# Plain-fp32 first units, a PE-built bias, a GpSimd causal mask and PE-made weight halves in an attention + maxout kernel

## The chip, the cores and the metric

One core of one Trainium2 chip runs the whole program in one launch. The metric is device microseconds of that core, as the median of several executions. Engines are written as in the profile: PE (TensorE matmul; PEld its weight loads), DVE (VectorE), ACT (ScalarE), POOL (GpSimd), SP (SyncE, which here issues nearly all DMAs).

## What is computed

Causal attention with a forget-gate bias for 8 batches of 8 heads, 576 positions of width 64, followed by a maxout feed-forward over 4608 tokens:

```
cum   = cumsum(max(s, 0))
bias  = min(-(cum[i] - cum[j]), 0)
score = q @ k.T / 8 + bias, and -1e9 where j > i
attn  = softmax(score);  x = attn @ v        # heads side by side: 4608 x 512
h     = max(x @ w1, x @ w2, x @ w3)          # 512 -> 768
out   = h @ w_out                            # 768 -> 512
```

The inputs q, k, v and s arrive as fp32; the weights arrive as float64 and are brought to fp32 words on the chip.

## The kernel before

**Units and steps.** Heads are handled in pairs `g` (four pairs per batch). The query rows of a batch are cut in five blocks `qb` (four of 128 rows and one of 64). A unit is a group of steps: "split" units (batches 0 to 3, two pairs, `qb` 0 and 1), "rest" units (the same batches, one pair, `qb` 2 to 4) and "whole" units (batches 4 to 7, one pair, all five). There are 8, 16 and 16 of them, 160 steps in all. Units 0 and 1 together make the first 256 rows of batch 0, and with them the first input `x` of the feed-forward.

**One step** (`one_step`, L727). PE forms the scores of both heads as three products of rounded parts, `qh·kh + ql·kh + qh·kl` (L752, fp32r), and adds the causal mask with one more matmul per head, `identb` times `tri` (L756). DVE subtracts the bias and takes the row minimum in one instruction (L796); ACT takes the exponential and the row sum (L805); ACT and DVE make the reciprocal (L812, L818). The normalized probabilities are split in two f16 halves, ACT the high one (L841) and DVE the low one (L849). SP transposes them by DMA (L861). After the last step of a phase PE multiplies with the halves of v (L904), and ACT or DVE write the halves of `x` (L930, L932, L937).

**What a unit needs first.** `qk_in` (L640) loads q and k (`qr`), rounds them on ACT (`qh`, L696), subtracts on DVE for the first five units and on POOL later (`ql`, L709), and loads the bias rows (`bias`, L686) spread over all partitions from `cd`, a DRAM copy of the cumulative sums. `cd` is made at the start: load `s` (L303), maximum (L337), scan (L342), centre and scale (L349), write to DRAM (L355). `values_split` (L605) makes the halves of v (ACT L618, DVE L623).

**Weights.** 24 tiles of 128 x 512: 18 for the three up products, 6 for the down product, taken in chunks of three (the last six together). Per tile: one ACT and two DVE instructions that turn the float64 words into fp32 (L423, L427, L431), a share in a Gram product on PE (L446) from which a power of two is derived in a chain of small DVE operations per chunk (L456 to L478), and two f16 halves: the high one by ACT (L514), the low one by DVE (L521).

**Experts** (`experts`, L948). One per batch and phase, 16 in all, each with 18 up groups of 12 matmuls (L981) whose results DVE, ACT and POOL turn into `h` (L992 to L1016), and 4 down groups of 18 (L1037).

**Order.** A planner (`Plan`) holds prices per operation and a key; it simulates the five engines and writes each engine's instruction order from that. Attention steps have the step number as key, weights `PACE[0]*i + PACE[1]`, and the experts a key so large that PE turns to them when no attention work is ready. PSUM holds two score tiles, one `av` tile and three `m` tiles; `p` and `pr` have two buffers each. Every engine runs its list in order; the semaphores follow the true dependences of each instruction. In the planner's own picture every POOL operation, and those of DVE marked as locking, exclude each other.

Of the kernel before, what the change touches and what calls it, by code (L numbers as in the profile page):

```python
# [20 lines left out]
PACE = (1.2, 0.0, 2200.0)  # L21
EARLY = 5
EARLYSET = 0
LOOK = (4.0, 10.0, 3.0, 3.5)
# [28 lines left out]
class Plan:  # L53
# [47 lines left out]
    def run(self):  # L101
# [15 lines left out]
        while left:  # L117
# [9 lines left out]
            for e in engines:  # L127
# [3 lines left out]
                while wait[e]:  # L131
# [4 lines left out]
                    held = pair > now and (e == "POOL" or e == "DVE" and op.lock)  # L136
# [16 lines left out]
                if e == "POOL" or e == "DVE" and op.lock:  # L153
                    pair = op.end
                    heapq.heappush(events, (pair, 1, 0, None))
# [27 lines left out]
def kernel(  # L183
# [8 lines left out]
    nc = tc.nc  # L192
# [26 lines left out]
        sc=6, am=3, vs=5, ws=3, os=4, s=2, av=1, m=3,  # L219
# [72 lines left out]
    ident = inner("ident", 16 * S, 4 * P)  # L292
# [27 lines left out]
    def do(e):  # L320
        nc.gpsimd.memset(tri4(), 0.0)
        for j in range(2):
# [8 lines left out]
        {"DVE": dve(128)},  # L331
        lambda e: nc.vector.tensor_scalar(out=identb(), in0=ident(), scalar1=1.0 / VSC, scalar2=None, op0=ALU.mult),
        -1000.0, [ident], [identb],
    )
    add(
        {"DVE": (451.0, 370.0)},
        lambda e: nc.vector.tensor_scalar(out=rt_()[0:HB], in0=st()[0:HB], scalar1=0.0, scalar2=None, op0=ALU.max),  # L337
        -1000.0, [st], [rt_],
    )
    add(  # L340
        {"DVE": (1350.0, 1270.0)},
        lambda e: nc.vector.tensor_tensor_scan(  # L342
            out=ct()[0:HB], data0=rt_()[0:HB], data1=rt_()[0:HB], initial=0.0, op0=ALU.add, op1=ALU.max
        ),
        -1000.0, [rt_], [ct],
    )
# [40 lines left out]


# [11 lines left out]
    def weights(c):  # L400
# [80 lines left out]
        if c == NFT:  # L481
# [23 lines left out]
            )  # L505
        for i in ids:
# [12 lines left out]

            def lo(e, r=r, w=w, sc=sc):  # L520
# [10 lines left out]
    units = [("split", b, (2 * h, 2 * h + 1), (0, 1)) for b in range(NB) for h in range(NP // 2)]  # L531
    units += [("rest", b, (g,), (2, 3, 4)) for b in range(NB) for g in range(NP)]
    units += [("whole", b, (g,), (0, 1, 2, 3, 4)) for b in range(NB, B) for g in range(NP)]
# [71 lines left out]
    def values_split(u):  # L605
        kind, b, gs, qbs = units[u]
        n = 512 if kind == "split" else 640
        rv, vs = RV.pop(u), VS[b, kind]
# [31 lines left out]
    def qk_in(u):  # L640
# [3 lines left out]
        hi = buf("qh", name=f"qh{u}")  # L644
        lo = buf("ql", name=f"ql{u}")
        bias = buf("bias", name=f"bias{u}")
        QK[u] = dict(lo=lo, hi=hi, bias=bias)
# [33 lines left out]
        def spread(e):  # L681
# [8 lines left out]
        load(  # L690
            spread, k - LOOK[2], 4 * P * nb_ * rows_, [cd], [bias], queue="ACT" if u == 0 else "SP", lat=2500.0,
        )
        for part, c0, c1 in parts:
# [37 lines left out]
    def one_step(u, a, g, qb, t, r, part, pT, tT):  # L731
        kind, b, gs, qbs = units[u]
        hi = lambda: r["hi"]().bitcast(F32R)
        lo = lambda: r["lo"]().bitcast(F32R)
        if kind == "split":
            qo, ko = 512 * a, 512 * a + 256
        else:
            qo, ko = 0, QP
# [4 lines left out]
        def scores(e):  # L743
            ps = sp().rearrange("p (a n) -> p a n", a=2)
            h, l = hi(), lo()
            if qb < 4:
                qs = slice(qo + qb * P, qo + qb * P + P)
                ks = slice(ko, ko + nk)
                for n, (lt, rt) in enumerate(((h[:, qs], h[:, ks]), (l[:, qs], h[:, ks]), (h[:, qs], l[:, ks]))):
                    for j in range(2):  # L750
                        rs = slice(D * j, D * j + D)
                        nc.tensor.matmul(  # L752
                            ps[:, j, :nk], lhsT=lt[rs], rhs=rt[rs], start=(n == 0), stop=False, skip_group_check=True
                        )
                for j in range(2):
# [16 lines left out]
        cost = (606.0, 673.0, 848.0, 1019.0, 938.0)[qb]  # L772
        add(
            {"PE": (cost + 100.0, cost)}, scores, t, [(r["hi"], part), (r["lo"], part), identb, tri, tri4], [sp]
        )
# [14 lines left out]

        for j in range(2):
# [5 lines left out]
                    out=pj(c)[rs], in0=src(c)[rs], in1=bias(j)[rs], scale=-SCALE, scalar=3.0e38, op0=ALU.add,  # L797
# [322 lines left out]
```

## Time and profile before

| | us |
|---|---|
| median of 3 executions (lowest, highest) | 856.57 (855.74, 857.03) |
| the profiled execution: its time | 857.28 |
| its span | 855.5 |
| PE busy | 808.5 (95%) |
| DVE busy | 603.5 (71%) |
| ACT busy | 544.5 (64%) |
| POOL busy | 168.3 (20%) |

The profile was taken in one execution whose time stands 1.8 us above its span. "Busy" is the union of the instructions of an engine; because matmuls are pipelined, a run of them is better read by the distance from one start to the next than by the mean of one.

### The profile page before, as it was taken

The numbers are of one execution on the slowest core, as the hardware profiler recorded it, in microseconds if no ns is written. First come the engines' busy times: TensorE is split into PE (matmuls) and PEld (weight loads), VectorE is DVE, ScalarE is ACT, GpSimd is POOL, SyncE is SP. The second block draws the span as 40 slices with busy tenths as digits, with TensorE's granted clock in tenths as the row PEclk, the third lists the DMA queues.
The fourth block names the chain that finished last, engine by engine and source line by source line (L and its number), as shares of the span: only waits on it lengthen the run. The fifth ranks groups of instructions, "written<-read, shape, count | busy, mean of one in ns | idle before, by whom it ended". The sixth has DMA issues, their size and how long they took to land.

```text
span 855.5 us, 19695 instructions
## 1 busy us (share of the span) xinstructions
PE 808.5 (95%) x7251; PEld 618.2 (72%) x7251; DVE 603.5 (71%) x1757; ACT 544.5 (64%) x1422; POOL 168.3 (20%) x177
## 2 busy tenths in 40 slices
PE   2558999999999999999999999999999999999998
PEld 1336878788887776777776788767877778778875
DVE  4998988777787878867767776687768768652221
ACT  3777877777776776776666766667676766751111
POOL 0000322222231312312222222221211222011110
PEclk9999999999999999999999999999999999999999
DMA  9887965899888888887765767676686655440000
GB/s 336 219 222 185 230 165 133 177 203 176 207 178 200 187 196 193 191 215 167 154 147 141 167 133 147 142 149 150 138 172 148 142 121 107 100 76 32 8 19 32
DMA packets 243216, 132.66 MB, mean 155 GB/s; under 512 B 211248, under 2 KB 225584, under 8 KB 243120
## 3 DMA queue, kind: packets, MB, share of 16 engines
q1 hardware_dynamic: 242432, 130.59, 66.7%
q8 instruction: 57, 0.93, 0.5%
q10 hardware_dynamic: 688, 0.82, 0.3%
q14 instruction: 39, 0.32, 0.2%
HBM read 70.40 MB, written 9.58 MB: 93 GB/s over the span
## 4 chain that ended last, share of the span: by engine, by line
PE 87%; DVE 6%; DMA 3%; issue 2%; ACT 1%; ACTq 0%; DVEq 0%
PE u L981 48%; PE d L1037 15%; PE s L752 9%; PE av L904 8%; PE s L764 3%; PE s L756 3%; DVE pr L849 2%; DMA bias<-cd 1%; DMA pT<-pr 1%; DVE p L796 1%; DMA cd<-early 1%; PE m L446 1%; DMA early<-in_s_dram 1%; DVE m L1004 0%; DVE ql L709 0%
## 5 line engine op out<-in xcount | busy, mean ns | idle before, releaser
L981 PE MATMUL u<-x,w 128*128 128x256 f16 (+1 forms) x3456 | 444.8, 287 | 0.1
L981 PEld LDWEIGHTS <-w 128*128 128x128 f16 x3456 | 333.1, 98 | 81.9 <-issue 0.3
L805 ACT ACTIVATE p<-p,sc 128x384 f32<-128x384 f32 (+4 forms) x288 | 166.1, 578 | 80.0 <-DVE sc L796 78.8
L849 DVE SCALAR_TENSOR_TENSOR pr<-p,sc,pr 128x384 f16<-128x384 f32 (+3 forms) x288 | 166.6, 595 | 31.9 <-ACT pr L841 31.0
L1016 POOL TENSOR_TENSOR h<-m,h 128x256 f16<-128x256 f32 (+1 forms) x96 | 72.9, 760 | 514.4 <-ACT h L1011 514.1
L796 DVE CUSTOM_DVE_ANT_0 p<-s,bias 128x512 f32<-128x512 f32 (+4 forms) x320 | 165.3, 537 | 8.0 <-DMA bias<-cd 3.7
L841 ACT ACTIVATE pr<-p,sc 128x384 f16<-128x384 f32 (+3 forms) x288 | 151.4, 568 | 22.1 <-DMA pT<-pr 16.3
L1004 DVE SCALAR_TENSOR_TENSOR m<-u,m 128x256 f32<-128x256 f32 (+1 forms) x192 | 87.3, 455 | 90.3 <-PE u L981 84.5
L1037 PE MATMUL d<-h,w 128*128 128x256 f16 (+1 forms) x1152 | 148.4, 286 | 0.0
L1037 PEld LDWEIGHTS <-w 128*128 128x128 f16 x1152 | 110.6, 98 | 27.0
L709 POOL TENSOR_TENSOR ql<-qr,qh 128x384 fp32r<-128x384 f32 (+2 forms) x70 | 94.0, 1363 | 160.7 <-issue 100.9
L1011 ACT ACTIVATE h<-m 128x256 f16<-128x256 f32 (+1 forms) x96 | 42.2, 439 | 100.3 <-DVE m L1004 99.5
L904 PE MATMUL av<-pT,vv 128*64 128x320 f16 (+3 forms) x1152 | 77.0, 280 | 2.5 <-DMA pT<-pr 2.5
L904 PEld LDWEIGHTS <-vv 128*64 128x64 f16 x1280 | 63.2, 112 | 22.3 <-issue 12.9
L752 PE MATMUL s<-qh 64*128 64x128 f32 (+3 forms) x256 | 55.4, 428 | 17.8 <-ACT qh L696 9.0
L1048 ACT ACTIVATE o<-d,os 128x256 f32<-128x256 f32 (+1 forms) x64 | 31.6, 494 | 47.2 <-PE d L1037 43.8
L996 DVE TENSOR_SCALAR m<-u 128x256 f32<-128x256 f32 (+1 forms) x58 | 26.4, 455 | 42.9 <-PE u L981 41.1
L752 PEld LDWEIGHTS s<-qh 64*128 64x128 f32 x256 | 25.5, 194 | 41.3 <-issue 21.5
L805 ACT ACTIVATION_READ_ACCUMULATOR p<-p,sc 128x1 f32 x288 | 54.1, 188 | 0.0
L696 ACT ACTIVATE qh<-qr 128x960 fp32r<-128x960 f32 (+3 forms) x41 | 43.8, 1069 | 6.3 <-DMA qr<-in_qkv_dram 2.4
L752 PE MATMUL s<-qh,ql 64*128 64x128 f32 (+3 forms) x256 | 43.5, 335 | 2.4 <-DVE ql L709 2.4
L818 DVE RECIPROCAL sc<-sc 128x2 f32<-128x2 f32 (+1 forms) x160 | 25.1, 158 | 28.7 <-ACT sc L812 27.8
(81 smaller groups left out, 655.5 us busy)
## 6 DMA issues: line engine op xcount, KB each, us to landing
bias<-cd SPq DMA_DIRECT2D x32, 576.0 KB, 4.7
rv<-in_qkv_dram SPq DMA_DIRECT2D x32, 320.0 KB, 3.9
qr<-in_qkv_dram SPq DMA_DIRECT2D x16, 608.0 KB, 4.2
raw<-in_w_dram SPq DMA_DIRECT2D x16, 512.0 KB, 5.6
qr<-in_qkv_dram SPq DMA_DIRECT2D x16, 480.0 KB, 3.8
out_dram<-o SPq DMA_DIRECT2D x32, 160.0 KB, 2.1
early<-in_w_dram SPq DMA_DIRECT2D x8, 512.0 KB, 6.3
out_dram<-o SPq DMA_DIRECT2D x32, 128.0 KB, 2.6
```

The costliest lines, as they stand in the source:

```text
L696: lambda e, c0=c0, c1=c1: nc.scalar.activation(out=hi().bitcast(F32R)[:, c0:c1], in_=raw()[:, c0:c1], func=AF.Copy),
L709: lambda e, d0=d0, d1=d1: E[e].tensor_tensor(out=lo().bitcast(F32R)[:, d0:d1], in0=raw()[:, d0:d1], in1=hi()[:, d0:d1], op=ALU.subtract),
L752: nc.tensor.matmul(ps[:, j, :nk], lhsT=lt[rs], rhs=rt[rs], start=(n == 0), stop=False, skip_group_check=True)
L796: lambda e, j=j, rs=rs, c=c: nc.vector.tensor_tensor_reduce(out=pj(c)[rs], in0=src(c)[rs], in1=bias(j)[rs], scale=-SCALE, scalar=3.0e38, o ...
L805: lambda e, j=j: nc.scalar.activation(out=pj(j), in_=pj(j), func=AF.Exp, scale=-1.0, bias=nm()[:, j:j + 1], accum_out=sm()[:, j:j + 1]),
L841: lambda e, h_=h_, s_=s_, j=j: nc.scalar.activation(out=h_(), in_=s_(), func=AF.Copy, scale=ri()[:, j:j + 1]),
L849: lambda e, h_=h_, l_=l_, s_=s_, j=j: nc.vector.scalar_tensor_tensor(out=l_(), in0=s_(), scalar=ri()[:, j:j + 1], in1=h_(), op0=ALU.mult, ...
L904: nc.tensor.matmul(av()[j * D:(j + 1) * D, c0:nq], lhsT=lt, rhs=rt, start=(n < 2), stop=(n >= len(todo) - 2), skip_group_check=True,)
L981: nc.tensor.matmul(pm()[:, :nq], lhsT=v[:, wt, kt, :], rhs=x(xt, kt), start=(k == 0), stop=(k == 3 * NKT - 1),)
L1004: lambda e, pm=pm, m1=m1: nc.vector.scalar_tensor_tensor(out=m1()[:, :nq], in0=pm()[:, :nq], scalar=HSC, in1=m1()[:, :nq], op0=ALU.mult, o ...
L1016: lambda e, m1=m1, ft=ft: E[e].tensor_tensor(out=h(1, ft), in0=m1()[:, :nq], in1=h(0, ft), op=ALU.subtract),
L1037: nc.tensor.matmul(pm()[:, :nq], lhsT=v[:, wt, dt, :], rhs=h(c, ft), start=(k == 0), stop=(k == 3 * NFT - 1))
```

## The change

- **First three units (`ND = 3`) in plain fp32.** Scores are one fp32 product of the raw q and k; there is no `qh`, `ql` or split v for these units. The probabilities stay unnormalized in fp32. POOL makes a diagonal matrix with the reciprocals (`pr = ident * ri`), and PE multiplies each probability block with it, which transposes and normalizes at once; ACT or DVE copies the result from PSUM (`turned`). The product with v is fp32 as well, and its scale goes into the `x` evictions.
- **Bias of units 0 and 1 (`NPB = 2`) by PE.** The scan is cut at column 256; the first 256 columns, centred, are `near`; PE spreads each row over the partitions with a one-column lhsT of `ident`, and ACT copies it. The other units load from `cd` as before.
- **Causal mask from unit 4 on (`MASKU = 4`, `qb < 4`) by GpSimd.** An `affine_select` on POOL writes the masked bias into the `p` tile; L796 then reads it there; the two mask matmuls of the step go.
- **Low halves of weight tiles 6 to 17 (`LOPE`) by PE.** A diagonal of the negated scale times the raw fp32 words, plus the f16 identity times the high half, in one `m` tile; ACT copies it. The DVE instruction L521 of these tiles goes.
- **Orders.** Weights get later keys; q and k are asked for 10 steps ahead instead of 4; the low part of `h` is made by DVE for the first two experts; the small scaling of the sums (L812) may go to DVE; the down groups of the first two output tiles are cut so that the last sixth of `h` is used in a part of its own; unlocked POOL operations no longer exclude others in the planner's picture. `ident` and the new small tiles live in the second `pT1` buffer.

```diff
-PACE = (1.2, 0.0, 2200.0)
+PACE = (1.6, -2.0, 1500.0)
-EARLYSET = 0
-LOOK = (4.0, 10.0, 3.0, 3.5)
+EARLYSET = 2
+LOOK = (10.0, 10.0, 4.0, 1.5)
+ND = 3
+NPB = 2
+MASKU = 4
+LOPE = (6, 18)
...
-                    held = pair > now and (e == "POOL" or e == "DVE" and op.lock)
+                    held = pair > now and op.lock and e in ("POOL", "DVE")
...
+    spans(0, 2 * P)
     add(
+        {"DVE": dve(256, 150.0, 1.0)},
+        lambda e: nc.vector.tensor_scalar(
+            out=near()[0:HB], in0=ct()[0:HB, 0:2 * P], scalar1=ct()[0:HB, P:P + 1], scalar2=1.0 / SCALE,
+            op0=ALU.subtract, op1=ALU.mult,
+        ),
+        -1000.0, [(ct, 0)], [near],
     )
+    spans(2 * P, S)
...
+            if LOPE[0] <= i < LOPE[1]:
...
+                def less(e, r=r, w=w, dg=dg, m=m):
+                    nc.tensor.matmul(m(), lhsT=dg(), rhs=words(r)[0], start=True, stop=False)
+                    nc.tensor.matmul(m(), lhsT=identh().bitcast(F16), rhs=w()[:, 0], start=False, stop=True)
+
+                add({"PE": (1300.0, 1200.0)}, less, k, [r, dg, identh, (w, 0)], [m])
+                add(
+                    {"ACT": act(N, PSI)},
+                    lambda e, w=w, m=m: nc.scalar.activation(out=w()[:, 1], in_=m(), func=AF.Copy, scale=-1.0),
+                    k - 0.3, [m], [(w, 1)],
+                )
+                continue
...
+        if u < NPB:
+            for i in range(0, nb_, 2):
+                m = buf("m", free=True)
+
+                def ones(e, m=m, i=i):
+                    for j in range(2):
+                        r = r0 + i + j
+                        nc.tensor.matmul(
+                            m()[:, j * rows_:(j + 1) * rows_], lhsT=ident()[0:HB, r:r + 1].to_broadcast([HB, P]),
+                            rhs=near()[0:HB], start=True, stop=True,
+                        )
+
+                add({"PE": (1300.0, 1200.0)}, ones, FIRST, [ident, near], [m])
...
+                if direct:
+                    terms = ((h[:, qs], h[:, ks]),)
+                else:
+                    terms = ((h[:, qs], h[:, ks]), (l[:, qs], h[:, ks]), (h[:, qs], l[:, ks]))
...
-                for j in range(2):
+                for j in range(0 if masked else 2):
                     nc.tensor.matmul(
                         ps[:, j, qb * P:nk], lhsT=identb(), rhs=tri(), start=False, stop=True, skip_group_check=True
                     )
...
-        cost = (606.0, 673.0, 848.0, 1019.0, 938.0)[qb]
+        cost = ((380.0, 460.0, 630.0, 800.0, 938.0) if masked else (606.0, 673.0, 848.0, 1019.0, 938.0))[qb]
+        if direct:
+            cost += 54.0 * (qb + 1)
...
+            def mask(e):
+                nc.gpsimd.affine_select(
+                    out=pt().rearrange("p (j n) -> p j n", j=2)[:, :, 0:nk],
+                    in_=r["bias"]()[:, 2 * a * w:2 * (a + 1) * w].rearrange("p (j n) -> p j n", j=2)[:, :, 0:nk],
+                    pattern=[[0, 2], [-1, nk]], compare_op=ALU.is_ge, fill=NEG, base=qb * P, channel_multiplier=1,
+                )
+
+            add({"POOL": (127.0 + 2.6 * nk, 100.0 + 2.6 * nk)}, mask, t - 0.5, [r["bias"]], [(pt, 0), (pt, 1)])
...
+    def turned(t, qb, pt, pr, sc, ri, pT):
...
+                lambda e, j=j: nc.gpsimd.tensor_scalar(
+                    out=pr()[:, j * P:(j + 1) * P], in0=ident(), scalar1=ri()[:, j:j + 1], scalar2=None, op0=ALU.mult
+                ),
...
+                for kb in range(qb + 1):
+                    nc.tensor.matmul(
+                        m()[:, (2 * kb + j) * P:(2 * kb + j + 1) * P],
+                        lhsT=pt()[:, 512 * j + kb * P:512 * j + (kb + 1) * P], rhs=pr()[:, j * P:(j + 1) * P],
+                        start=True, stop=True,
+                    )
+
+            add({"PE": (400.0 * (qb + 1), 350.0 * (qb + 1))}, turn, t, [(pt, j), (pr, j)], [(m, j)])
...
-        cost = 1654.0 if ph else 618.0
+        cost = 1654.0 if ph else 1700.0 if direct else 618.0
...
+            cut = NFT - 1 if dt < 2 else NFT
+            for f0, f1 in ((0, cut), (cut, NFT)):
+                if f0 < f1:
+                    add(
+                        {"PE": (3 * (f1 - f0) * mm + 100.0, 3 * (f1 - f0) * mm)},
+                        lambda e, down=down, f0=f0, f1=f1: down(e, f0=f0, f1=f1),
+                        base + 50 + dt + (2 if dt > 1 or f0 else 0),
```

More of the change, by code (lines that the diff above doesn't have):

```diff
@@ L152, in run @@
                 free[e] = now + busy
-                if e == "POOL" or e == "DVE" and op.lock:
+                if op.lock and e in ("POOL", "DVE"):
                     pair = op.end
@@ L386, in power @@
         )
+    for n in range(2):
+        seed = Buf(plan, "dg", None, "order")
+        seed.ops.extend(near.ops)
     W = {}
@@ L528 @@
         weights(c)
[L531 to L533 removed]
+    units = []
+    for o in ORDER:
+        b = int(o[1])
+        if o[0] == "s":
+            units += [("split", b, (2 * h, 2 * h + 1), (0, 1)) for h in range(NP // 2)]
+        elif o[0] == "r":
+            units += [("rest", b, (g,), (2, 3, 4)) for g in range(NP)]
+        else:
+            units += [("whole", b, (g,), (0, 1, 2, 3, 4)) for g in range(NP)]
     begin = []
@@ L688, in spread @@
                 )
[L690 to L693, printed above, removed]
+        if u < NPB:
+            for i in range(0, nb_, 2):
+                m = buf("m", free=True)
+                def ones(e, m=m, i=i):
[4 more added lines that the diff above has]
+                            rhs=near()[0:HB], start=True, stop=True,
+                        )
+                add({"PE": (1300.0, 1200.0)}, ones, FIRST, [ident, near], [m])
+                add(
+                    {"ACT": act(2 * rows_, PSI)},
+                    lambda e, m=m, i=i: nc.scalar.activation(
+                        out=bias()[:, i * rows_:(i + 2) * rows_], in_=m()[:, 0:2 * rows_], func=AF.Copy
+                    ),
+                    FIRST, [m], [(bias, i)],
+                )
+        else:
+            load(spread, k - LOOK[2], 4 * P * nb_ * rows_, [cd], [bias], lat=4500.0 if u < 4 else 2500.0)
+        for part, c0, c1 in parts if u >= ND else ():
             add(
@@ L734, in one_step @@
         lo = lambda: r["lo"]().bitcast(F32R)
+        direct, masked = u < ND, u >= MASKU and qb < 4
         if kind == "split":
@@ L770, in scores @@
                 )
-        cost = (606.0, 673.0, 848.0, 1019.0, 938.0)[qb]
-        add(
-            {"PE": (cost + 100.0, cost)}, scores, t, [(r["hi"], part), (r["lo"], part), identb, tri, tri4], [sp]
-        )
+        cost = ((380.0, 460.0, 630.0, 800.0, 938.0) if masked else (606.0, 673.0, 848.0, 1019.0, 938.0))[qb]
+        if direct:
+            cost += 54.0 * (qb + 1)
+        ins = [(r["raw"], part)] if direct else [(r["hi"], part), (r["lo"], part)]
+        add({"PE": (cost + 100.0, cost)}, scores, t, ins + [identb, tri, tri4], [sp])
         pt = buf("p", name=f"p{t}")
@@ L809, in one_step @@
             )
+        psc = 1.0 if direct else 1.0 / PSC
         add(
-            {"ACT": (204.0, 110.0)},
+            {"ACT": (204.0, 110.0), "DVE": (145.0, 65.0)},
             lambda e: nc.scalar.activation(
-                out=se()[:, :nj], in_=sm()[:, :nj], func=AF.Copy, scale=1.0 / PSC, bias=EPS / PSC
+                out=se()[:, :nj], in_=sm()[:, :nj], func=AF.Copy, scale=psc, bias=EPS * psc
+            )
+            if e == "ACT"
+            else nc.vector.tensor_scalar(
+                out=se()[:, :nj], in0=sm()[:, :nj], scalar1=psc, scalar2=EPS * psc, op0=ALU.mult, op1=ALU.add
             ),
```

141 lines of the change are left out of this document (105 added, 36 removed).

## The prediction

> **What bounds the kernel now.** I read the slices of the span first, then windows by stage, then the waits and the timeline of the start.
>
> ```profile
> span 855.5 us, 19695 instructions
> ...
> PE   2558999999999999999999999999999999999998
> ...
> DVE  4998988777787878867767776687768768652221
> ```
>
> Forty slices of 21.4 us, busy share in tenths. PE is full from the fifth slice on, and not in the first four; DVE is full in just those. Windows put numbers to it (columns: stretch, length, then busy us and count of PE, PEld, DVE, ACT, POOL, then clock, DMA share, GB/s).
>
> ```profile
> 0.00:25.00 25.00, 6.04 (x39) 3.92 (x39) 12.14 (x33) 8.02 (x18) 1.71 (x11) 1.00 0.93 326
> 25.00:70.00 45.00, 23.63 (x171) 16.11 (x172) 44.13 (x155) 36.27 (x98) 0.00 (x0) 1.00 0.85 219
> ...
> 140.00:745.00 605.00, 602.26 (x5485) 457.88 (x5482) 454.09 (x1278) 424.27 (x1096) 136.62 (x131) 1.00 0.74 163
> ```
>
> So two stages. Up to 70 us PE is busy 29.7 us of 70, while DVE works 44.13 of the 45 us from 25 on: the start is bound by DVE, and before 25 by something else. From 140 to 745 PE is busy 602.26 of 605: there only removed PE work shortens anything. The timeline of the start names the early bound:
>
> ```profile
> 5.39 0.45 DVE L337 TENSOR_SCALAR early<-early 64x576 f32<-64x576 f32 x1 [3.83 <-DMA early<-in_s_dram]
> ...
> 14.68 0.42 ACTq L686 DMA_DIRECT2D bias<-cd  x1
> ...
> 23.08 0.29 DVE L796 CUSTOM_DVE_ANT_0 p<-s,bias 128x128 f32<-128x128 f32 x1 [3.70 <-DMA bias<-cd]
> ```
>
> The sums go to DRAM and back; the first softmax starts at 23.08. On PE the stage ends here (the same rows serve below):
>
> ```profile
> 69.92 2.77 PE L981 MATMUL u<-x,w 128*128 128x256 f16 x12
> ...
> 80.91 0.69 PE L904 MATMUL av<-pT,vv 128*64 128x256 f16 x12
> 81.53 0.33 PE L752 MATMUL s<-qh 64*128 64x128 f32 x2
> 81.69 0.28 PE L752 MATMUL s<-qh,ql 64*128 64x128 f32 x2
> 81.80 0.27 PE L752 MATMUL s<-ql,qh 64*128 64x128 f32 x2
> 82.01 0.28 PE L756 MATMUL s<-tri,identb 128*128 128x128 bf16 x2
> 82.13 1.47 PE L981 MATMUL u<-x,w 128*128 128x256 f16 x12
> ...
> 84.21 1.11 PE L446 MATMUL m<-raw 128*128 128x128 bf16 x8
> ```
>
> The first expert starts at 69.92, when units 0 and 1 (eight steps) have given the first `x`. From then on PE always has expert work. Hence the account: the time is the moment at which the first expert can start, plus the PE work still to be done then, plus the end.
>
> **The change part by part.** The sum is made against the profiled execution (857.28 us, span 855.5), 0.7 above the median of 856.57.
>
> *A. When the first expert starts.* `s` still lands at 5.39. On 256 columns the maximum, scan and centring should take about 1 us, two fp32 products and one ACT copy per pair of rows 2 to 4 us: first softmax near 9.5 instead of 23.08. What DVE then has to do is read from its groups between 23 and 69.9 us (count, busy us, mean ns):
>
> ```profile
> L849 DVE SCALAR_TENSOR_TENSOR pr<-p,sc,pr 128x128 f16<-128x128 f32 (+1 forms) x20 | 8.0, 411 | 0.1
> L796 DVE CUSTOM_DVE_ANT_0 p<-s,bias 128x128 f32<-128x128 f32 (+1 forms) x22 | 6.9, 347 | 3.7 <-DMA bias<-cd 3.7
> L521 DVE SCALAR_TENSOR_TENSOR w<-raw,sws,w 128x512 f16<-128x512 f32 x8 | 5.9, 742 | 0.0
> L709 DVE TENSOR_TENSOR ql<-qr,qh 128x512 fp32r<-128x512 f32 x8 | 5.3, 684 | 0.2 <-ACT qh L696 0.2
> L427 DVE TENSOR_SCALAR early<-early 128x512 int32<-128x512 int32 x11 | 4.6, 416 | 0.0
> L431 DVE SCALAR_TENSOR_TENSOR raw<-raw,early 128x512 int32<-128x512 int32 x5 | 3.4, 689 | 0.1
> ...
> L576 DVE TENSOR_REDUCE am<-rv 128x1 f32<-128x512 f32 x5 | 3.4, 674 | 0.0
> ```
>
> The old stage is 69.92 - 23.08 = 46.8 us of full DVE. Of it go, for good in these units, the low halves of the probabilities (8.0) and of q and k (5.3). Put off by the later keys until after the first `x`: 7 of 11 weight conversions (7 x (0.416 + 0.689) = 7.7), half of the 12 low weight halves (6 x 0.742 = 4.5), 3 of 11 softmax steps (6 x 0.347 = 2.1), two of five maxima (1.3) and two scale chains, by my estimate 1.5. That is 30.4 us less: 16.4. Added: the copies of the transposed blocks, half of them on ACT; the nearest row is an eviction of 256 columns,
>
> ```profile
> L932 DVE TENSOR_SCALAR x<-av 128x256 f16<-128x256 f32 x14 | 5.9, 418 | 3.2 <-PE av L904 3.0
> ```
>
> so 4 pairs x (0.42 + about 0.7) / 2 = 2.2; and the early work that used to lie in the wait before 23.08: of the 12.14 us before 25, some 7 (three conversions, two maxima, a scale, the second half of the scan). Together 25.6 us, so at the earliest 9.5 + 25.6 = 35; with some 5 us for chains that the two `p` buffers don't cover, I take **40**. Gain 29.9. Bounds: 33, if chains are covered, and 55, if PE limits (first rival). ACT loses more than it gains there (qh, high halves of p and v against the bias and pT copies), and was busy 36.27 of 45: cover. DMA: q and k of unit 1 are asked for earlier in the same queue and land ahead of later weights.
>
> *B. PE work that the old kernel had behind it at 69.92 and the new one will not have at 40.* Scores of five more steps (82.13 - 81.53 = 0.60 each, 3.1 with the wider blocks) and Gram products of about five weights (1.11 / 2 each, 2.5). Cost 5.6.
>
> *C. Low weight halves by PE, 12 tiles, nearly all after 40 us, in the PE-bound stage.* Per tile an fp32 product of 512 columns and an f16 one. No plain-fp32 matmul is in the trace. Nearest are fp32r pairs of 512 columns, and mask positions:
>
> ```profile
> 189.06 0.39 PE L752 MATMUL s<-qh,ql 64*128 64x512 f32 x2
> 189.28 0.40 PE L752 MATMUL s<-ql,qh 64*128 64x512 f32 x2
> ...
> 196.63 0.28 PE L756 MATMUL s<-tri,identb 128*128 128x128 bf16 x2
> 196.76 5.40 PE L981 MATMUL u<-x,w 128*128 128x256 f16 x48
> ```
>
> One pass of 512 columns takes 0.22. Lower bound: fp32 goes like fp32r, 0.44 per tile, 5.3 in all. Upper: an fp32 product is four products of halves (the kernel makes three of them), 4 x 0.22 + 0.22 = 1.1, 13.2 in all. I take the upper end, since the planner prices it at 1.2, and where its prices can be compared they are good: 618 ns for `av` against 81.53 - 80.91 = 0.62, 606 for a step against 0.60. Cost 13.5. DVE loses 12 x 0.742, ACT gains about as much; neither is the bound there. The Trainium skill (FP8 and Floating Point Precision, TensorE Precision Notes) says that true fp32 takes four passes through the array; an estimate from it would be the same 13.2, and no run here shows it yet.
>
> *D. Unit 2, direct, after 40 us* (units 0 and 1 lie in A, where PE idles). Per pair: scores +0.16 by the planner; six 128-column fp32 products for turning, 2.1 by the planner, from six single passes (0.7) to four passes each (2.9); `av` 1.7 against 0.62. Two pairs: cost 6.7, bounds 1 to 9. The diagonal on POOL, idle until 75 us, is free.
>
> *E. The causal mask leaves PE.*
>
> ```profile
> L756 PE MATMUL s<-tri,identb 128*128 128x128 bf16 x256 | 38.0, 233 | 0.0
> ```
>
> The 38.0 busy overstates it; start to start the two matmuls take 0.13 (196.63 to 196.76) or 0.12 (82.01 to 82.13). The longer wait ahead of them (81.80 to 82.01 against 0.11 between pairs) belongs to the change from half to full array height; I expect the next `u` to inherit it. Masked steps: 16 in split units, 32 in rest, 64 in whole = 112; gain 112 x 0.13 = 14.6. If the wait goes too, 0.23 each, 25.8. POOL pays instead:
>
> ```profile
> masks.py:199 POOL TENSOR_SCALAR_AFFINE_SELECT early<-early 128x128 f32<-128x128 f32 x1 | 0.3, 292 | 0.1
> L324 POOL TENSOR_SCALAR_AFFINE_SELECT tri<-tri 64x64 bf16<-64x64 bf16 x2 | 0.5, 234 | 0.1
> ...
> L709 POOL TENSOR_TENSOR ql<-qr,qh 128x576 fp32r<-128x576 f32 x32 | 45.2, 1414 | 0.0
> L709 POOL TENSOR_TENSOR ql<-qr,qh 128x384 fp32r<-128x384 f32 x16 | 16.5, 1030 | 67.7 <-issue 40.4 <-ACT qh L696 27.0 <-POOL h L1016 0.3
> ```
>
> By the first two rows 0.9 ns per element over 0.18, 88 us in all; by the last two 2.0 over 0.26, 181 us. With 168 us of its own POOL stays below half; `ql` and `h` queue behind a mask that waits for its `p` buffer, so `h` may come a step late, hidden while PE has other groups.
>
> *F. Weights behind the first expert.* Its 18 up groups ask for tiles faster than DVE delivers them; the gap is filled by C, D and later units. I put 4 us of new PE idling, bounds 0 to 12. The cut down groups, L812's choice and `EARLYSET` change order, not PE work: at 842 us the last down groups follow the last up groups without a gap already, so 0; without that cover a wait of one `h` chain, about 2 us.
>
> Sum: -29.9 + 5.6 + 13.5 + 6.7 - 14.6 + 4 = -14.7. 857.3 - 14.7 = 842.6, as a median about **842**.
>
> **Rivals.**
>
> 1. *Slower: plain fp32 on a slow array binds the start.* Before 75 us PE runs at half rate although the granted clock reads 1.00:
>
> ```profile
> 70.13 2.56 PE u L981 x12
> ...
> 79.67 1.31 PE u L981 x12
> ```
>
> PE work up to the first `x`, at planner prices: bias 4 x 1.2, scores 5.8, turning 4 x 2.1, `av` 4 x 1.7, Gram 3.5, together 29 us; at 2.56 / 1.31 that is 57, from about 7 us on: first expert at 64, time 842 + 24 = 866. It decides from a first expert at 55 on. Against it: an array that is busy without gaps speeds up within 4 us (the two rows), so this limits itself. The Trainium skill (TensorE: Matmul & The Clock Gate, Part 1) says the same, that a sustained busy window releases the full clock. Chance 0.12.
>
> 2. *Slower: the mask holds attention back.* DVE is seen blocked: L849 takes up to 1617 ns at a median of 608.
>
> ```profile
> L849 DVE SCALAR_TENSOR_TENSOR pr<-p,sc,pr x288: 332/608/1617, 27.0 to 761.2; 128x512 f16<-128x512 f32 x48, 128x128 f16<-128x128 f32 x32, 128x256 f16<-128x256 f32 x32, 128x384 f16<-128x384 f32 x32
> ```
>
> The Trainium skill (SBUF — State Buffer, SBUF: two separate sides) makes this an exclusive lock between GpSimd and a DVE operation with two SBUF inputs; the new planner picture leaves the mask out of it. But attention has slack:
>
> ```profile
> 771.26 1.65 PE av L904 x28
> ...
> 782.63 25.69 PE L981 MATMUL u<-x,w 128*128 128x256 f16 x228
> ```
>
> The last `x` is there at 774; its expert starts after 18 of the 19 groups of the last row, at 807. So 33 us may be lost, 0.3 per masked step. At 0.5 per step: 56 - 33 = 23 us, 865. Chance 0.06.
>
> 3. *Weights late.* The last tile's key goes from 27.6 to 34.8, seven steps later, at the rate of 40 to 70 us about 15 to 20 us; if the down groups wait for it for 10 us more, 852. Chance 0.17.
>
> 4. *Cheaper than priced.* The array-height wait goes with the mask (-11), or fp32 costs near one pass (-14 in C and D), or the first expert starts at 33 (-7): 826 to 831. Chance 0.20.
>
> **How the numbers follow.** Forecast (832 to 851) 0.45. Rivals 1 and 2 beyond the range are 0.18; rival 4 reaches to 825, rival 3 to 856. Range 825 to 857. A measurement here can tell about 0.2% (1.7 us). Faster: forecast 0.45, rival 4 0.20, most of rival 3 0.14, the mild part of 1: 0.03, so 0.82; same 0.05; slower 0.13.
>
> **What would show it.** First softmax at 8 to 11 us; first `u` at 33 to 48; DVE still full, POOL not above 350 us; low-half groups on PE about 1.1 us start to start, or near 0.4 if fp32 is cheap; the position of L756 taken by `u` 0.2 after the last pair (wait inherited) or 0.1 (gone); PE still full from 140 to 745. A first `u` after 55, or a PE hole between 90 and 150 or after 745, makes the prediction wrong.

## The result, and the profile after

| | before | after |
|---|---|---|
| median (lowest, highest; runs) | 856.8 (855.74, 857.34; 4) | 836.32 (835.97, 837.25; 4) |
| profiled execution: span | 855.5 | 834.4 |
| PE busy | 808.5 | 818.3 |
| DVE busy | 603.5 | 622.6 |
| POOL busy | 168.3 | 266.7 |

The changed kernel takes 0.9764 of the time of the one before, 95% interval 0.9747 to 0.9781: 20.5 us less, where 14.7 were forecast. The slices of the span, as they were read before:

```profile
span 834.4 us, 19417 instructions
...
PE   7889999999999999999999999999999999999998
...
DVE  5899989788888878877788876877878775774231
```

Each slice is 20.9 us here. In the kernel before PE began with 2, 5, 5 and 8 tenths, beside DVE's 4, 9, 9 and 8; now PE begins with 7, 8 and 8 and is full from the fourth slice on. DVE is as busy as it was, but PE no longer waits beside it. The windows of the changed kernel, in the columns of the prediction's, say the same, and the last two cut the span at the first expert:

```profile
0.00:25.00 25.00, 19.54 (x85) 13.80 (x85) 14.32 (x54) 11.21 (x31) 6.22 (x19) 1.00 0.81 285
25.00:70.00 45.00, 39.81 (x279) 26.83 (x280) 41.33 (x163) 37.74 (x99) 13.69 (x20) 0.96 0.72 234
...
140.00:745.00 605.00, 603.02 (x5373) 456.65 (x5372) 474.82 (x1320) 400.09 (x972) 214.43 (x225) 1.00 0.73 158
```

```profile
0.00:49.58 49.58, 39.76 (x230) 28.04 (x230) 36.98 (x143) 30.76 (x83) 14.82 (x32) 0.97 0.72 245
49.58:834.00 784.42, 778.56 (x6876) 592.04 (x6874) 585.63 (x1699) 494.60 (x1224) 251.88 (x273) 1.00 0.67 149
```

The kernel before, cut at its own first expert:

```profile
0.00:69.92 69.92, 29.60 (x208) 19.95 (x208) 56.19 (x187) 44.21 (x115) 1.71 (x11) 1.00 0.88 258
69.92:855.00 785.08, 778.90 (x7046) 598.25 (x7044) 547.30 (x1571) 500.33 (x1308) 166.63 (x166) 1.00 0.66 146
```

The stage after the first expert's start is 784.42 us long against 785.08, and PE is busy 778.56 of it against 778.90. So as bookkeeping nearly all of the gain (20.3 of the span's 21.1) is the earlier start, 49.58 instead of 69.92, and what was added to PE behind it cancels what was taken away. What the bookkeeping can't say is what each part is worth; the experiments give another picture of that.

The start on the changed kernel's timelines, of PE first and then of ACT and DVE (start, length, operation, and in brackets the idle time ahead and what ended it):

```profile
7.18 7.19 PE L770 MATMUL m<-early 64*128 64x256 f32 x16
...
17.19 3.35 PE L1020 MATMUL m<-pr,p 128*128 128x128 f32 x12
...
24.14 2.05 PE L1020 MATMUL m<-pr,p 128*128 128x128 f32 x12
...
47.75 1.29 PE L1020 MATMUL m<-pr,p 128*128 128x128 f32 x8 [0.29 <-POOL pr L1010]
...
49.58 1.47 PE L1143 MATMUL u<-x,w 128*128 128x256 f16 x12
50.89 1.06 PE L573 MATMUL m<-early,early 128*128 128x512 f32 x2
51.79 0.38 PE L574 MATMUL m<-w,early 128*128 128x512 f16 x1
52.10 0.87 PE L1063 MATMUL av<-pT,rv 128*64 128x256 f32 x8
```

```profile
11.71 0.66 ACT L459 ACTIVATE early<-raw 128x512 f32<-128x512 f32 x1 [1.83 <-DMA raw<-in_w_dram]
...
12.41 0.43 DVE L463 TENSOR_SCALAR early<-early 128x512 int32<-128x512 int32 x1 [4.00 <-ACT early L459]
13.48 0.29 DVE L909 CUSTOM_DVE_ANT_0 p<-s,bias 128x128 f32<-128x128 f32 x1
```

The bias is on the partitions early (8 fp32 products from 7.18 on, which the profile records as two matmuls each, x16; the first copy by ACT at 9.29), yet the first softmax starts at 13.48. DVE stood 4.00 us at L463, a weight conversion that the planner had put ahead of it in DVE's list; L463 waited for ACT's L459, and that for the first weight tile's DMA. An engine that runs its list in order waits for the first item of it, even where the second is ready.

### The profile page after: what moved, and what is told of

It is laid out like the page before. It is cut to its first block, busy times and chain, and to the rows that moved or that the text cites. A ratio compares the mean times of both kernels' runs of the same rounds, so it can differ in the third digit from the quotient of the medians.

```text
span 834.4 us, 19417 instructions
## 1 busy us (share of the span) xinstructions
PE 818.3 (98%) x7103; PEld 620.1 (74%) x7103; DVE 622.6 (75%) x1841; ACT 525.4 (63%) x1306; POOL 266.7 (32%) x305
## 5 line engine op out<-in xcount | busy, mean ns | idle before, releaser
L1143 PEld LDWEIGHTS <-w 128*128 128x128 f16 x3456 | 329.4, 98 | 98.1 <-issue 14.1
L970 DVE SCALAR_TENSOR_TENSOR pr<-p,sc,pr 128x384 f16<-128x384 f32 (+3 forms) x264 | 158.1, 617 | 22.6 <-ACT pr L962 22.1
L897 POOL TENSOR_SCALAR_AFFINE_SELECT p<-bias 128x768 f32<-128x768 f32 (+1 forms) x112 | 88.3, 789 | 230.3 <-DVE pr L970 157.2
L962 ACT ACTIVATE pr<-p,sc 128x384 f16<-128x384 f32 (+3 forms) x264 | 141.7, 579 | 25.9 <-DMA pT<-pr 9.1
L1178 POOL TENSOR_TENSOR h<-m,h 128x320 f16<-128x320 f32 (+1 forms) x84 | 64.1, 764 | 219.3 <-ACT h L1173 219.3
L909 DVE CUSTOM_DVE_ANT_0 p<-s,p 128x384 f32<-128x384 f32 (+1 forms) x224 | 106.8, 502 | 10.9 <-POOL p L897 10.6
L1063 PE MATMUL av<-pT,vv 128*64 128x320 f16 (+3 forms) x1080 | 71.0, 277 | 0.0
L909 DVE CUSTOM_DVE_ANT_0 p<-s,bias 64x576 f32<-64x576 f32 (+2 forms) x96 | 58.6, 618 | 2.2 <-PE m L1020 0.6
L930 DVE TENSOR_SCALAR sc<-sc 128x2 f32<-128x2 f32 (+1 forms) x111 | 32.8, 295 | 25.5 <-ACT p L918 23.8
L852 PE MATMUL s<-qh 64*128 64x384 f32 (+1 forms) x232 | 47.7, 407 | 1.2 <-DVE sc L909 1.0
L788 ACT ACTIVATE qh<-qr 128x960 fp32r<-128x960 f32 (+2 forms) x37 | 40.5, 1095 | 6.4 <-PE s L869 5.5
```

Source lines behind the costliest of these rows:

```text
L852: nc.tensor.matmul(ps[:, j, :nk], lhsT=lt[rs], rhs=rt[rs], start=(n == 0), stop=(masked and n == len(terms) - 1), skip_group_check=True,)
L897: nc.gpsimd.affine_select(out=pt().rearrange("p (j n) -> p j n", j=2)[:, :, 0:nk], in_=r["bias"]()[:, 2 * a * w:2 * (a + 1) * w].rearrange ...
L909: lambda e, j=j, rs=rs, c=c: nc.vector.tensor_tensor_reduce(out=pj(c)[rs], in0=src(c)[rs], in1=(pj(c) if masked else bias(j))[rs], scale=- ...
L962: lambda e, h_=h_, s_=s_, j=j: nc.scalar.activation(out=h_(), in_=s_(), func=AF.Copy, scale=ri()[:, j:j + 1]),
L970: lambda e, h_=h_, l_=l_, s_=s_, j=j: nc.vector.scalar_tensor_tensor(out=l_(), in0=s_(), scalar=ri()[:, j:j + 1], in1=h_(), op0=ALU.mult, ...
L1063: nc.tensor.matmul(av()[j * D:(j + 1) * D, c0:nq], lhsT=lt, rhs=rt, start=(n < 2), stop=(n >= len(todo) - 2), skip_group_check=True,)
```

## The experiments

A frame first, found while reading the runs. In several of them PE is busy without a gap from batch 4's expert on and has a hole just ahead of it. The order of the units explains the place: split units (32 steps) and rest units (48) feed two experts per batch; the 16 steps after the 80th bring no new expert input, and only the 97th completes the first rows of batch 4. The store of expert work that PE falls back on is lowest there. So the table has, for each run, the first `u` of the first expert, the first `u` of batch 4 (the ninth expert's), and the span; and as a measure of attention the moments at which its 8th, 40th and 96th step is done, counted by the reciprocals on DVE (one per step, 160 in all).

| run | step 8 | first `u` | step 40 | step 96 | steps 40 to 96 | `u` of batch 4 | span | span less `u` of batch 4 |
|---|---|---|---|---|---|---|---|---|
| before | 56.0 | 69.9 | 200.8 | 471.8 | 271.0 | 487.0 | 855.5 | 368.5 |
| after | 39.3 | 49.6 | 176.6 | 456.4 | 279.9 | 470.8 | 834.4 | 363.6 |
| no mask part | 39.0 | 49.3 | 175.0 | 448.8 | 273.8 | 485.7 | 849.3 | 363.6 |
| no weight halves by PE | 39.2 | 49.6 | 192.5 | 472.5 | 279.9 | 489.6 | 852.9 | 363.3 |
| no fp32 units | 50.1 | 65.2 | 196.0 | 478.6 | 282.6 | 494.1 | 857.1 | 363.0 |
| no bias by PE | 48.5 | 73.5 | 192.6 | 472.9 | 280.3 | 492.4 | 857.0 | 364.6 |
| mask part alone | 57.3 | 71.2 | 198.6 | 481.3 | 282.7 | 497.5 | 860.8 | 363.3 |
| mask done twice | 38.8 | 50.1 | 182.7 | 473.5 | 290.7 | 489.3 | 865.5 | 376.2 |

### One part undone at a time

Four kernels, each with one part of the change off. Each is planned anew, so the order of the rest moves too.

The mask goes back to PE:

```diff
-MASKU = 4
+MASKU = 99
```

> The changed kernel with the mask back on PE for all units (MASKU beyond the last unit), all else kept. Theory A (the account: time = moment of the first expert + PE work after it): first expert unmoved at about 50 us, PE gets 224 mask matmuls back, 15 to 18 us more, 851 to 854. Rival (the mask on GpSimd slows attention and so gave part of its gain back): less than 10 us more, under 846.

Measured: 850.71 (850.27 to 851.1), 0.9932 [0.9917, 0.9947]; 14.4 slower than the change as a whole. The part's price on PE, 14.6, comes back almost to the figure. PE is full in this run (39.79 of the 40 us from 460 to 500) and takes batch 4's input 37 us after step 96, against 14 in the changed kernel: attention is ahead, and PE alone sets the time.

The low weight halves go back to DVE:

```diff
-LOPE = (6, 18)
+LOPE = (0, 0)
```

> The changed kernel with all low weight halves by DVE again (LOPE empty). Theory A: PE is the bound from the first expert on, so the 14.5 us of PE work (12 tiles of 1.2 us) go straight off, 821 to 826. Rival (DVE feeds PE with weight tiles between 50 and 100 us, and needs the relief): PE idles instead, 833 to 842.

Measured: 855.74, 0.9991 [0.9981, 1.0001]; 19.4 slower, although PE has some 14.5 us less to do. I had expected this part to cost. The windows of this run:

```profile
50.00:140.00 90.00, 86.21 (x817) 70.90 (x815) 86.21 (x300) 67.90 (x198) 27.04 (x33) 0.98 0.77 199
140.00:460.00 320.00, 309.47 (x2692) 231.06 (x2692) 257.24 (x667) 212.52 (x489) 108.44 (x112) 0.99 0.78 170
460.00:500.00 40.00, 29.58 (x237) 22.17 (x234) 27.25 (x92) 25.27 (x63) 12.25 (x12) 0.79 0.77 164
```

PE loses 3.8 us from 50 to 140, where DVE has 86.21 us of work instead of the change's 82.58; then 10.5 us up to 460 and 10.4 in the 40 us behind it, in which the granted clock falls to 0.79. PE is out of work, not overloaded. Attention comes late: steps 40 and 96 are done 15.9 and 16.0 us later than in the changed kernel. The last low half leaves DVE late as well, as the same last operation on the two timelines of DVE shows, here and in the changed kernel:

```profile
155.98 0.74 DVE L585 SCALAR_TENSOR_TENSOR w<-early,rels,w 128x512 f16<-128x512 f32 x1
```

```profile
140.13 0.74 DVE L585 SCALAR_TENSOR_TENSOR w<-early,rels,w 128x512 f16<-128x512 f32 x1
```

From 50 to 140 DVE is busy 86.21 of 90 us; the 12 halves of 0.742, 8.9 us, come back as a delay of some 16, and PE meets it as a hole at batch 4. The delay is larger than the work that was given back; the planner also wrote another order here, and the two are not split.

The first units in split parts again, and the bias by way of DRAM again:

```diff
-ND = 3
+ND = 0
```

> The changed kernel with no plain-fp32 unit (ND = 0), bias of units 0 and 1 still by PE. Theory A: the first expert moves from 50 to about 60 us, since low halves of q, k, v and of the probabilities come back to DVE and the DMA transposes to the chain; PE work after it hardly changes: 843 to 850. Rival (the direct path costs as much on PE and GpSimd as it saves on DVE): 832 to 840.

```diff
-NPB = 2
+NPB = 0
```

> The changed kernel with the bias of all units loaded from DRAM (NPB = 0). Theory A: the first softmax goes from 13.5 to about 22 us and the first expert with it by 5 to 9 us: 841 to 845. Rival (the 7 us that PE takes for the bias and the in-order wait for the first weight tile give the head start away): within 2 us of the changed kernel, 834 to 838.

Measured: 858.37, 1.0023 [1.0008, 1.0038], first expert at 65.2; and 858.85, 1.0032 [1.002, 1.0045], first expert at 73.5. Each of the two takes away the whole gain and a little more. Their delays of step 8 (10.9 and 9.3 us) stand as 22.2 and 16.5 at step 96. Without the bias part the timeline of PE shows the hole and its cause:

```profile
488.80 0.47 PE L852 MATMUL s<-qh 64*128 64x128 f32 x2 [5.76 <-DVE sc L909]
...
492.39 0.82 PE L1143 MATMUL u<-x,w 128*128 128x256 f16 x3
```

PE waits 5.76 us for DVE's softmax step to free a score tile; it has no expert work to fall back on. The worths of the four parts, undone one by one, are 14.4, 19.4, 22.1 and 22.5: 78 us in all, of a change that is worth 20.5. They don't add, as would be expected of two limits that lie close together.

### The order kept, one cost changed

Here the planned order is that of the changed kernel, instruction by instruction, and one operation is changed in it.

The fp32 product of the low halves is left out; the f16 one stays.

```diff
-                    nc.tensor.matmul(m(), lhsT=dg(), rhs=words(r)[0], start=True, stop=False)
-                    nc.tensor.matmul(m(), lhsT=identh().bitcast(F16), rhs=w()[:, 0], start=False, stop=True)
+                    nc.tensor.matmul(m(), lhsT=identh().bitcast(F16), rhs=w()[:, 0], start=True, stop=True)
```

> The changed kernel in its own instruction order, but the low weight halves of the 12 tiles leave out the fp32 product (12 times about 0.9 us of PE, 10.9 us; what is left is the f16 product and the copy). Theory A (PE work after the first expert is the bound): 825 to 827. Theory B (the first input of batch 4 is the bound: PE has used up all expert work when it comes, at 470.8 us, so PE work taken out before that is only waited away): 832 to 837.

Measured: 836.31 (836.03 to 839.44), 0.9775 [0.9755, 0.9796]: no change, for 12 x 0.90 = 10.8 us of PE work less. The windows say where it went, first this kernel and then the changed one (this kernel's profile is of its slowest execution, 839.44; the other three lie between 836.03 and 836.37):

```profile
50.00:140.00 90.00, 81.33 (x728) 64.16 (x727) 79.82 (x300) 70.80 (x196) 25.37 (x33) 0.92 0.71 189
140.00:460.00 320.00, 319.54 (x2828) 240.81 (x2825) 262.93 (x695) 221.41 (x517) 117.67 (x120) 1.00 0.82 180
```

```profile
50.00:140.00 90.00, 89.14 (x776) 67.57 (x775) 82.58 (x312) 74.42 (x208) 26.85 (x34) 1.00 0.76 200
140.00:460.00 320.00, 319.51 (x2821) 240.29 (x2820) 260.96 (x686) 220.32 (x512) 116.59 (x119) 1.00 0.82 179
```

From 50 to 140 PE is busy 81.33 instead of 89.14: it idles for most of the time it saved, with nothing ready for it, and its granted clock is 0.92. PE's share looks full in the changed kernel, but PE isn't the limit in that stage: this much of its work can go without a gain.

The mask is done twice, the second time writing the same again:

```diff
             def mask(e):
-                nc.gpsimd.affine_select(
+                for _ in range(2):
+                    nc.gpsimd.affine_select(
```

> The changed kernel in its own instruction order, with the mask made twice on GpSimd (112 more affine selects, 88 us of GpSimd, 0.79 us each in the chain of a masked step). Theory A with the slack of 33 us that the prediction read at the end of the span: 836 to 840. Theory B (attention has no slack at the first input of batch 4): of 61 masked steps before it a good part of 0.4 to 0.8 us each is passed on, 850 to 875.

Measured: 866.78, 1.0126 [1.0111, 1.0141]: 30.5 slower for 90 us more on POOL (356.7 against 266.7), 0.27 us for each of the 112 masked steps. POOL is busy 41% of the span, and it still passes a third of its extra time on. PE's waits in this run:

```profile
PE s L852 <- DVE sc L910: 21.3, 29, 1.9
```

21.3 us in 29 waits of at most 1.9, where the changed kernel has 2.6 in 6: PE runs out of work in many places, from 140 to 460 (308.87 us busy of 320) and behind batch 4's `u` too (376.2 us to the end instead of 363.6). DVE's waits for the mask, in the changed kernel and then in this one, show the path:

```profile
DVE p L909 <- POOL p L897: 10.6, 17, 1.1
```

```profile
DVE p L910 <- POOL p L898: 54.1, 69, 1.8
```

The softmax step stands and waits for the mask, 54.1 us in all. Step 8, ahead of the first masked step, is unmoved (38.8 for 39.3); step 40 is 6.1 us late and step 96 17.0. In the table the steps from 40 to 96 take 271.0 and 273.8 us with the mask on PE, 279.9 to 282.7 with it on POOL and 290.7 with it there twice. That is what the mask costs attention, and attention has no slack for it.

### The same question with another order of units

> The changed kernel with the units in another order: after the split units, whole batches and rest batches alternate (w4, r0, w5, r1, w6, r2, w7, r3), so that the 17 steps without a new expert input fall where experts are still in store. Theory A: PE was full anyway, 833 to 837. Theory B: the same, as both bounds were level in the changed kernel, and PE's idle time after the first expert was only 2.8 us: 832 to 837. A loss (over 845) would say that the alternation makes a wait of its own.

> The alternated order and all low weight halves by DVE. Theory B: without the hole at batch 4 most of the 14.5 us of PE work shows, 821 to 829. Rival (the relief of DVE is needed before that: weights and attention both come late between 50 and 200 us): 835 to 850.

```diff
-ORDER = ("s0", "s1", "s2", "s3", "r0", "r1", "r2", "r3", "w4", "w5", "w6", "w7")
+ORDER = ("s0", "s1", "s2", "s3", "w4", "r0", "w5", "r1", "w6", "r2", "w7", "r3")
```

With whole and rest units in turn there is no long stretch without a new expert input. The first kernel has only this edit, the second also `LOPE = (0, 0)`. Measured: 837.66 (836.12 to 840.17), 0.9786 [0.9763, 0.9808], and 851.72, 0.9948 [0.9931, 0.9965]. The order by itself brings nothing. Without the halves by PE the loss is 14.1 here, after 19.4 above, and the idle time is spread (19.6 us behind the first expert against 4.2, of it 6.7 between 200 and 300). Step 40 is 17.6 us later than in the alternated order alone (195.1 for 177.5). So batch 4 is where the delay of attention comes to light; most of the loss is the delay, not the place.

### The mask alone

```diff
-PACE = (1.6, -2.0, 1500.0)
+PACE = (1.2, 0.0, 2200.0)
...
-EARLYSET = 2
-LOOK = (10.0, 10.0, 4.0, 1.5)
-ND = 3
-NPB = 2
+EARLYSET = 0
+LOOK = (4.0, 10.0, 3.0, 3.5)
+ND = 0
+NPB = 0
...
-LOPE = (6, 18)
+LOPE = (0, 0)
```

What stays of the change is the mask on POOL, the cut down groups, the choice of engine for L812 and the planner's picture of locks; no run splits the mask from the other three.

> Of the change only the GpSimd mask (and the cut down groups, the free place of the small scaling and the planner's new picture of locks); direct units, PE bias, PE weight halves, keys and look-ahead as before. If the parts add up: 14 us below the kernel before, 841 to 844. Theory B (attention without slack sets the pace as well as PE; the mask takes time from PE but adds to attention's steps, and only an earlier start lets both gain): 850 to 862.

Measured: 863.3, 1.008 [1.0065, 1.0095]: 6.7 us **slower** than before, with 14.6 us less for PE to do. Its window of the ebb and its timeline of PE there:

```profile
460.00:500.00 40.00, 28.22 (x225) 20.75 (x222) 27.30 (x88) 25.75 (x62) 11.98 (x11) 0.76 0.74 154
```

```profile
480.40 0.69 PE L852 MATMUL s<-qh 64*128 64x384 f32 x2 [4.93 <-DVE sc L909]
```

PE idles 11.8 of 40 us. Step 40 is done 2.2 us earlier than in the kernel before and step 96 is 9.5 later, 11.7 lost in between. What is left of the change buys PE 14.6 us and costs attention about 10; without a head start the second decides.

### Attempts to improve on it

Three edits aimed at what the profile shows as waits in the changed kernel.

The planner is told that the first three weight tiles land later (6 us after issue, not 2), so that DVE doesn't stand at L463:

```diff
-                k - 6.0, 8 * P * N, writes=[r], begin=max(0.0, PACE[2] * (i - 3)),
+                k - 6.0, 8 * P * N, writes=[r], begin=max(0.0, PACE[2] * (i - 3)), lat=6000.0 if i < 3 else 2000.0,
```

> The changed kernel with the planner told that the first three weight tiles land later (6 us for 2), so that DVE and ACT don't stand behind the first tile's landing at 11.7 us before the first softmax. First softmax at 10 to 11 us for 13.5, first expert 2 to 3 us earlier. Theory A and B alike: 832 to 836; a time above 838 would say that the first 14 us aren't what sets the first expert.

Measured: 840.46, 0.9811 [0.9796, 0.9825]; 4.1 slower. The first softmax moves to where it was forecast, on this kernel's timeline of DVE:

```profile
9.53 0.29 DVE L909 CUSTOM_DVE_ANT_0 p<-s,bias 128x128 f32<-128x128 f32 x1 [1.50 <-ACT bias L778]
```

and the first expert to 44.7, 4.9 earlier. But batch 4's `u` is at 474.6, 3.8 later than in the changed kernel. Step 8 is done 2.2 us earlier (37.0), step 40 3.0 later (179.6): the planner writes another order from there on. An earlier first expert is worth nothing if the steps behind it come later.

The diagonals of the reciprocals by ACT instead of POOL:

```diff
-                {"POOL": (290.0, 260.0)},
-                lambda e, j=j: nc.gpsimd.tensor_scalar(
-                    out=pr()[:, j * P:(j + 1) * P], in0=ident(), scalar1=ri()[:, j:j + 1], scalar2=None, op0=ALU.mult
+                {"ACT": (390.0, 300.0)},
+                lambda e, j=j: nc.scalar.activation(
+                    out=pr()[:, j * P:(j + 1) * P], in_=ident(), func=AF.Copy, scale=ri()[:, j:j + 1]
```

> The changed kernel with the diagonals of the direct units made by ACT instead of GpSimd (0.3 to 0.4 us for 0.6, twice per direct step, in the chain from the reciprocal to the transposing product). If this chain sets the first expert: some 8 steps times 0.4 us earlier, 832 to 835. If DVE and ACT are the bound there: the same or later, 836 to 842.

Measured: 841.99, 0.9831 [0.981, 0.9852]; 5.7 slower. First expert at 48.6, step 40 at 183.1, batch 4 at 475.5: the same pattern.

A third `p` buffer, paid for with one `tl` and one `m1` less:

```diff
-        qr=2, qh=2, ql=2, rv=4, vv=2, bias=2, p=2, pr=2, tl=2, pT0=2, pT1=2, tT=2, t=5, m1=3, o=2,
+        qr=2, qh=2, ql=2, rv=4, vv=2, bias=2, p=3, pr=2, tl=1, pT0=2, pT1=2, tT=2, t=5, m1=2, o=2,
```

> The changed kernel with three p buffers (paid for by one buffer less of the maxout partial results and of the small tail tile). The mask waits for a p buffer of two steps before (157 us of such waits on GpSimd in the changed kernel). If that wait is what the mask costs: it shrinks to under 80 us, attention is ahead, and the time is 831 to 836. If the missing maxout buffer matters more: 838 to 850.

Measured: 854.4, 0.9975 [0.9966, 0.9985]; 18.1 slower. The wait it was to shorten, by the waits of the changed kernel and then of this one:

```profile
POOL p L897 <- DVE pr L970: 157.2, 69, 6.4
```

```profile
POOL p L897 <- DVE pr L970: 197.7, 74, 6.9
```

It grew. Step 8 is done 5.5 us earlier than in the changed kernel (33.8), yet the first `u` comes 8.3 later (57.9) and step 96 10.5 later. The smaller buffers take part in this, and POOL now simply asks earlier, so the run says nothing about whether two `p` buffers are what the mask costs attention. No version here was faster than the changed kernel.

## Why the prediction was right, and where its steps failed

The forecast of 842 missed the time by 5.7 us, inside the 832 to 851 to which it gave the largest chance. The way to it was less good: two large errors offset, and that they did is luck. Of its signs, the first softmax (13.48 for 8 to 11) and the first `u` (49.58 for 33 to 48) came out later than named; POOL's 266.7 us, the 1.21 us of a low half on PE, the wait inherited by `u` and the full PE from 140 to 745 came out as named.

**A, the first expert at 40: mis-sized, 49.58.** The gain is 20.3, not 29.9. Four microseconds are the first softmax (13.48, not 9.5), by the weight conversion ahead of it in DVE's list; the run that moved it got 9.53 and 44.7. The step had counted DVE's work and not the order in which it stands. The other 5.6 lie in the stage itself, 36.1 us from softmax to expert for a forecast of 30.5. By the window from 13.48 to 49.58 DVE is busy 32.25 of it, where the step had counted 25.6 us of work; it idles 3.9, where 5 were put for uncovered chains. So the step had counted too little work on DVE. About one of the 5.6 us goes with the diagonals on POOL (first expert at 48.6 with them on ACT).

**B, 5.6 of PE work that the old kernel had behind it: mostly not there.** By the groups of PE's work behind the first expert, the two kernels have the same number of score products left, 230 matmuls of each of the three kinds on the 64-row lines L752 and L852. The changed kernel had no more of them done at 49.58 than the kernel before at 69.92, and no fewer. (Five weights at 1.11 / 2 would also have been 2.8, not 2.5.) Only the Gram products differ:

```profile
L482 PE MATMUL m<-raw 128*128 128x128 bf16 x40 | 5.4, 297 | 0.0
...
L482 PE MATMUL m<-early 128*128 128x128 bf16 x20 | 3.2, 296 | 0.0
```

60 of them against the 48 of before, 12 at 1.11 / 8 = 0.14 from start to start: 1.7 us.

**C, low halves on PE for 13.5: the price was right, the sign of its worth wrong.** From 50.89 to 51.79 the fp32 product takes 0.90, from there to 52.10 the f16 one 0.31: 1.21 per tile, 14.5 for twelve. The Trainium skill (FP8 and Floating Point Precision, TensorE Precision Notes) has true fp32 as four passes; the trace agrees, 0.90 for 4 x 0.22. What failed is the sentence that DVE and ACT are not the bound there. It was read from PE's window of 140 to 745; up to 140, where these halves are made, PE isn't the limit, and the runs fit DVE as the one that sets the pace, though none shows it alone. Leaving the fp32 product out gained nothing, and giving the halves back to DVE cost 19.4, or 14.1 in another order; in the first case attention is some 16 us late.

**D, unit 2 for 6.7: mostly spent before the first expert.** Its turning products are 24 matmuls, two for each fp32 product; 12 of them lie behind 49.58, at 2.05 / 12 = 0.17 each some 2 us. The price was right: six products take 2.05, for the planner's 2.1.

**E, the mask for -14.6: right in company of the other parts.** Undone there it costs 14.4; with hardly anything else of the change, the part loses 6.7. The wait that goes with the change of array height was inherited as forecast (that the height is its cause is argued, not tested); the changed kernel's timeline of PE at a masked step:

```profile
192.16 0.34 PE L852 MATMUL s<-ql,qh 64*128 64x384 f32 x2
192.43 1.49 PE L1143 MATMUL u<-x,w 128*128 128x256 f16 x12
```

0.27 us from the third pair to the next `u`. In the kernel before that stretch, from the row below to the mask at 196.63, was 0.26, and `u` came 0.13 behind the mask:

```profile
196.37 0.33 PE L752 MATMUL s<-ql,qh 64*128 64x384 f32 x2
```

POOL's price came out at the lower bound too:

```profile
L897 POOL TENSOR_SCALAR_AFFINE_SELECT p<-bias 128x768 f32<-128x768 f32 (+1 forms) x112 | 88.3, 789 | 230.3 <-DVE pr L970 157.2
```

**F, 4 us of new idling: not there.** Behind the first expert PE idles 784.42 - 778.56 = 5.9 us by the windows, 6.2 before.

Behind the first expert the terms were to add 15.2 us; they added nothing (C 14.5, B and D some 4, the mask -14.4; the rest, some -5, has in it the slow first groups of before, 2.77 us for the twelve matmuls that take 1.47 here, and isn't split further). That error and A's, 9.6, have opposite signs.

**The rivals.** The first, a slow array in the start, is there, and for longer than the prediction held possible: the spreading products take 7.19, and twelve turning matmuls 3.35 at 17.19 against 2.05 at 24.14. PE idles nowhere for as long as 0.15 us from 4.64 to 15.16, and still it is slow up to some 21 us. So the 4 us of gapless work that the prediction took for enough, with the rule cited beside them, were not enough here; apart from a few mask matmuls the work is of 64 rows until 17.00, and whether that decides was not tested. The first softmax waited for DVE and not for the array; what the slow array costs the stage behind it isn't measured. The first expert stayed short of the 55 from which this rival was to decide. The second, the mask holding attention back, failed by its slack: 33 us were read at the end of the span, where there is much expert work left (31, in fact: by its shape the last expert begins at 804.9, two groups ahead of the row's end); doubling the mask cost from the first masked units on. The slack that counts is that at batch 4, and there is none: in the changed kernel, on PE's timeline,

```profile
470.82 1.16 PE L1143 MATMUL u<-x,w 128*128 128x256 f16 x9
...
472.21 0.27 PE L1143 MATMUL u<-x,w 128*128 128x256 f16 x1 [0.24 <-DVE x L1094]
```

PE takes the ninth expert's first groups the moment their `x` exists, and waits 0.24 for the next. Its mechanism was not the one named either: the longest L970 (the old L849) takes 1947 ns for 1617 before, but all low halves of the probabilities together keep DVE busy for 168.8 us in the changed kernel and for 167.7 with the mask back on PE. The third, late weights, didn't occur: the last half is written at 140.13, 0.74 long, and none of PE's waits is for one of DVE's halves. Of the fourth, cheaper prices, none came true.

**What made the gain.** Two limits lie close together: all the work that PE has, and the moment at which attention delivers batch 4's first input, behind which come some 363 us of full PE. The mask's move takes 14.6 off the first and adds some 6 us (in company, steps 40 to 96) to 12 (alone) to the second; the fp32 units, the bias by PE and the halves by PE, with the new keys and look-ahead, bring attention forward (17 us at step 8, 24 at step 40) and add to the first. The mask part alone (with the three small edits left in that run) gives +6.7, all without it -5.7, both together -20.5. For the second limit speak the hole at batch 4 and the last column, 363.0 to 364.6, in four runs; the run without the mask part has the same figure with PE full, so it says nothing for it. Open are by what path the single mask slows the steps (DVE waits for POOL only 3.5 us from 140 to 460, where it waits 24.4 with the mask twice), why the steps behind an earlier start come later in the attempts, and what the new keys and look-ahead are worth: no run takes them out by themselves.

## What to carry to other kernels

Read the slack of a producer at the point where the busy engine's store of other work is lowest, not at the end of the span. An engine at 99% in a window is not thereby the limit of that window: take work off it in the same order and see whether it only idles instead. Where two limits lie close together, the parts of a change don't add, and a part that loses almost by itself (+6.7) can be needed for the gain of the whole.

## What was unexpected of the hardware

- The granted clock tells a slow array only where the trace has a record of it. The first group behind the hole of the mask-only kernel took 2.74, and a narrow window there reads 0.50 (timeline of PE, then the window):

```profile
497.52 2.74 PE L1143 MATMUL u<-x,w 128*128 128x256 f16 x12
```

```profile
497.50:500.00 2.50, 2.50 (x14) 1.79 (x13) 2.37 (x6) 0.87 (x3) 0.00 (x0) 0.50 0.90 239
```

The first group of the kernel before took 2.77 where the profile reads 1.00. But that trace's first clock record is at 74.5 us (at 22.6 in the changed kernel), and a stretch without a record is shown as 1.00. So the 1.00 ahead of it, which the prediction set against the half rate, is not a measurement.

- On GpSimd a tile times a per-partition number took more than twice the 0.29 us that the affine select of the same 128 x 128 shape took in the prediction's rows; by the changed kernel's groups:

```profile
L1010 POOL TENSOR_SCALAR pr<-early,sc 128x128 f32<-128x128 f32 x24 | 16.5, 700 | 36.1 <-DVE sc L936 14.6 <-DVE vs L399 14.0 <-DVE sc L930 4.9
```
